# K worked in two halves, and weights by one masked multiply on VectorE, in a one-token attention kernel

## The chip, the cores and the metric

One core of one Trainium2 chip. The metric is device time of one execution in microseconds (us).

## The reference

```python
B, H, Sq, Skv, Dh = 8, 32, 1, 4096, 128          # q, k, v in bf16
scores = jnp.einsum('bhqd,bhkd->bhqk', q, k) * Dh ** -0.5
attn = softmax(scores, axis=-1)
return jnp.einsum('bhqk,bhkd->bhqd', attn, v)
```

One query row for each of 256 heads. K and V are read once each: 2 x 256 x 4096 x 128 x 2 bytes = 537 MB, against hardly any arithmetic per byte.

## The kernel before

A tile is 8 heads; 16 partitions hold one head, and each partition holds C = 256 of its rows. There are 32 tiles. One K or V tile is 8.4 MB, and three buffers of that size are shared by K and V in turn:

```python
kv_pool = ctx.enter_context(tc.tile_pool(name="kv_pool", bufs=SLOTS))     # SLOTS = 3
...
nc.sync.dma_start(buf[:, c0 : c0 + n, :], src[t, :, c0 : c0 + n, :])      # load(): all from one queue
```

V of a tile goes into the buffer that K of the same tile had, so its load is issued when TensorE has made the last sum over that K. K of tile t+1 goes into the buffer of V of tile t-2.

Scores: VectorE (DVE) multiplies K by q in place and folds the 128 products of a row once or twice; TensorE adds the rest up with an identity matrix, and VectorE reduces what is left.

```python
nc.vector.tensor_tensor(out=part, in0=part, in1=qb[:].to_broadcast([P, hi - lo, D]), op=ALU.mult)
nc.vector.tensor_tensor(out=part[:, :, 0 : D // 2], ..., op=ALU.add)           # 128 -> 64
if width_of(t, lo // UC) < D // 2:
    nc.vector.tensor_tensor(out=part[:, :, 0 : D // 4], ..., op=ALU.add)       # 64 -> 32
...
for s in range(n):                                      # sum_over_d(): a quarter of K at a time
    nc.tensor.matmul(ps[:], lhsT=ident[:],
        rhs=kt[:, u * UC : (u + 1) * UC, s * DS : (s + 1) * DS], ...)          # UC = 64, DS = 8
```

Weights: after the maximum, ScalarE (ACT) makes the exponentials, then eight copies, one per head, each scaled by a column that is 1 on the partitions of that head and 0 elsewhere.

```python
nc.scalar.activation(out=e[:], in_=sc[:], func=ACT.Exp, bias=nmax[:, 0:1], scale=scale, ...)
for g in range(G):
    nc.scalar.activation(out=w[:, :, g, :], in_=e_g, func=ACT.Copy, scale=mine[:, 0, g : g + 1])
```

Values: 64 matmuls of those weights with V. In tiles 1 to 29 they run in a loop for the tile before, behind the sums. The first and the last two tiles are handled apart, in quarters of K.

## Time and profile before

| | before |
|---|---|
| time, median of 3 | 1251.89 us (1251.55 to 1251.96) |
| load queue busy | 99.5% of 16 DMA engines' span |
| VectorE busy | 1021.9 us, 82% |
| TensorE busy, its weight loads not counted | 786.8 us, 63% |
| ScalarE busy | 166.1 us, 13% |
| VectorE's wait for K | 139.9 us in 28 waits |

### The profile page before, as it was taken

The page shows a single profiled execution, that of the slowest core. Times are in us where ns is not written, and L with a number is a line of the kernel's source. Part 1 is how long each engine was busy: PE and PEld are TensorE (multiplying, and loading weights), DVE is VectorE, ACT ScalarE, POOL GpSimd, SP SyncE. Part 2 cuts the span into 40 slices and gives each one's busy share as a digit, 9 for nine tenths or more (in the row PEclk, how much of TensorE's full clock was granted, in tenths as well). Part 3 has the DMA queues.
Part 4 walks back from the last instruction along what each step waited for, and adds up shares of the span by engine and source line. Part 5 has one row for each costly group of instructions (what it writes and reads, how often), then busy time and mean ns, then how long its engine had stood idle before and what let it go on. Part 6 is the DMA issues. An engine that isn't in the chain of part 4 may idle for free. (4 is left out here: it accounts for less than half of the span.)

```text
span 1250.2 us, 10842 instructions
## 1 busy us (share of the span) xinstructions
PE 786.8 (63%) x3116; PEld 299.6 (24%) x3116; DVE 1021.9 (82%) x495; ACT 166.1 (13%) x433; POOL 4.5 (0%) x24
## 2 busy tenths in 40 slices
PE   3366567666576655766558665577655776556755
PEld 1122123222232222322223222222222222212222
DVE  7887987878977789777798777987779877798783
ACT  0111011111011110111101111011110111101111
POOL 1000000000000000000000000000000000000000
PEclk9987788777888778877788777887778878779867
DMA  9999999999999999999999999999999999999997
GB/s 405 436 436 435 434 436 432 436 430 428 426 437 436 429 435 434 434 435 436 436 434 432 424 437 437 432 430 428 436 437 434 430 433 434 430 435 421 427 446 329
DMA packets 11432, 537.33 MB, mean 430 GB/s; under 512 B 1808, under 2 KB 2064, under 8 KB 2320
## 3 DMA queue, kind: packets, MB, share of 16 engines
q1 hardware_dynamic: 11072, 536.94, 99.5%
q8 instruction: 15, 0.25, 0.1%
q10 hardware_dynamic: 336, 0.07, 0.0%
q14 instruction: 9, 0.07, 0.0%
HBM read 536.94 MB, written 0.07 MB: 430 GB/s over the span
## 5 line engine op out<-in xcount | busy, mean ns | idle before, releaser
L191 DVE TENSOR_TENSOR kt<-kt,qb 128x8192 bf16<-128x8192 bf16 (+1 forms) x99 | 560.9, 5665 | 146.6 <-DMA kt<-in_k_dram 139.9
L211 PE MATMUL ps<-kt,ident 128*128 128x512 bf16 x800 | 278.4, 511 | 389.9 <-DVE kt L199 299.7
L294 PE MATMUL av<-vt,w 128*32 x1740 | 425.5, 397 | 4.6
L194 DVE TENSOR_TENSOR kt<-kt 128x4096 bf16<-128x4096 bf16 (+1 forms) x99 | 288.8, 2917 | 3.4
L294 PEld LDWEIGHTS av<-vt,w 128*32 x1740 | 173.4, 100 | 262.4 <-issue 119.5
L211 PEld LDWEIGHTS <-ident 128*128 128x128 bf16 x800 | 95.7, 120 | 565.4 <-issue 527.9
L223 DVE TENSOR_REDUCE sc<-ps 128x64 f32<-128x512 f32 x128 | 85.3, 685 | 54.0 <-PE ps L211 54.0
L248 ACT ACTIVATE e<-sc,nmax 128x256 bf16<-128x256 f32 x32 | 16.3, 508 | 706.7 <-DVE nmax L242 706.7
L255 ACT ACTIVATE w<-e,mine 128x256 bf16<-128x256 bf16 x256 | 105.6, 495 | 1.1
L199 DVE TENSOR_TENSOR kt<-kt 128x2048 bf16<-128x2048 bf16 x56 | 68.6, 1225 | 1.9
L351 ACT ACTIVATE comb<-av 32x512 bf16<-32x512 f32 (+1 forms) x32 | 18.8, 586 | 329.0 <-PEq L284 321.4
L280 PE MATMUL av<-vt,w 128*32 128x512 bf16 x116 | 47.2, 499 | 14.6 <-issue 13.1
L371 PE MATMUL op<-comb,pick 32*16 32x128 bf16 (+1 forms) x128 | 12.1, 213 | 20.7 <-ACT comb L351 20.7
L280 PEld LDWEIGHTS av<-vt,w 128*32 128x32 bf16 x116 | 6.9, 100 | 55.2 <-issue 55.2
L177 PE MATMUL qp<-qg,heads 8*128 8x128 bf16 x32 | 7.0, 217 | 16.7 <-ACT qg L175 16.7
L371 PEld LDWEIGHTS <-pick 32*16 32x16 bf16 (+1 forms) x128 | 8.7, 83 | 27.7 <-issue 27.3
L322 PE MATMUL av<-vt,w 128*32 128x512 bf16 x188 | 13.7, 418 | 2.3 <-DMA vt<-in_v_dram 2.3
L235 DVE TENSOR_REDUCE pmax<-sc 128x1 f32<-128x256 f32 x32 | 13.4, 420 | 1.1
L175 ACT ACTIVATE qg<-qh 8x128 bf16<-8x128 f32 x32 | 8.5, 266 | 33.5 <-PE qh L171 33.5
L171 PE MATMUL qh<-q_all,ident 128*8 128x128 bf16 x32 | 7.2, 225 | 8.7 <-DMA q_all<-in_q_dram 8.3
L179 ACT ACTIVATE qb<-qp 128x128 bf16<-128x128 f32 x32 | 8.9, 278 | 9.7 <-PE qp L177 9.7
L237 DVE TENSOR_SCALAR spread<-same,pmax 128x32 f32<-128x32 f32 x32 | 7.7, 242 | 1.1
(31 smaller groups left out, 47.7 us busy)
## 6 DMA issues: line engine op xcount, KB each, us to landing
kt<-in_k_dram SPq DMA_DIRECT2D x4, 4096.0 KB, 24.3
kt<-in_k_dram SPq DMA_DIRECT2D x4, 2048.0 KB, 13.0
vt<-in_v_dram SPq DMA_DIRECT2D x1, 4096.0 KB, 33.9
vt<-in_v_dram SPq DMA_DIRECT2D x1, 2048.0 KB, 38.5
vt<-in_v_dram SPq DMA_DIRECT2D x1, 1024.0 KB, 40.5
vt<-in_v_dram SPq DMA_DIRECT2D x1, 512.0 KB, 41.3
vt<-in_v_dram SPq DMA_DIRECT2D x31, 25.8
kt<-in_k_dram SPq DMA_DIRECT2D x29, 28.3
```

What stands on the lines that cost most here:

```text
L191: nc.vector.tensor_tensor(out=part, in0=part, in1=qb[:].to_broadcast([P, hi - lo, D]), op=ALU.mult)
L194: nc.vector.tensor_tensor(out=part[:, :, 0 : D // 2], in0=part[:, :, 0 : D // 2], in1=part[:, :, D // 2 : D], op=ALU.add,)
L199: nc.vector.tensor_tensor(out=part[:, :, 0 : D // 4], in0=part[:, :, 0 : D // 4], in1=part[:, :, D // 4 : D // 2], op=ALU.add,)
L211: nc.tensor.matmul(ps[:], lhsT=ident[:], rhs=kt[:, u * UC : (u + 1) * UC, s * DS : (s + 1) * DS], start=(s == 0), stop=(s == n - 1),)
L223: made = nc.vector.tensor_reduce(out=scs[t][:, u * UC : (u + 1) * UC], in_=sums.pop((t, u))[:], axis=AX.X, op=ALU.add)
L248: nc.scalar.activation(out=e[:], in_=sc[:], func=ACT.Exp, bias=nmax[:, 0:1], scale=scale, accum_out=esums[t // R][:, t % R : t % R + 1],)
L255: nc.scalar.activation(out=w[:, :, g, :], in_=e_g, func=ACT.Copy, scale=mine[:, 0, g : g + 1])
L280: pe.matmul(av, lhsT=wf[:, i * nw : (i + 1) * nw], rhs=vf[:, i * nv : (i + 1) * nv], **how)
L294: pe.matmul(av, lhsT=wf[:, bass.ds(ow + i * nw, nw)], rhs=vf[:, bass.ds(ov + i * nv, nv)], start=False, stop=False,)
L322: nc.tensor.matmul(avs[t][j * AG : (j + 1) * AG, :], lhsT=w[:, i, :, :], rhs=vt[:, c0 : c0 + CB, :], start=(i < TG), stop=(j not in group[ ...
L351: nc.scalar.activation(out=comb[0:n, :, :], in_=av[0:n, :, :], func=ACT.Copy)
L371: nc.tensor.matmul(ops[n][:], lhsT=pick[0:e, m, r, :], rhs=comb[0:e, m, :], start=(r == 0 and m == 0), stop=(r == R - 1 and m == CB - 1 an ...
```

## The change

Its intent is to give the looped tiles fewer and longer instructions: the second half of K becomes one multiply with one more fold, so that each half needs one tile of sums (`ps`, 128 x 512, written by TensorE) and one reduction; and the eight copies on ScalarE become one instruction on VectorE.

```diff
-        return D // 4 if u >= NU // 2 and 0 < t < NT - 3 else D // 2
+        return D // 8 if lo == C // 2 and 0 < t < NT - 3 else D // 2
...
+    mask = consts.tile([P, G], BF16, name="mask")
+    nc.gpsimd.tensor_copy(out=mask[:], in_=mine[:, 0, 0:G])
...
-        for g in range(G):
-            nc.scalar.activation(
-                out=w[:, :, g, :], in_=e_g, func=ACT.Copy, scale=mine[:, 0, g : g + 1]
-            )
+        e_g = e_g.rearrange("p i (o m) -> p i o m", o=1).to_broadcast([P, C // CB, G, CB])
+        own_g = mask[:].rearrange("p (o g q) -> p o g q", o=1, q=1)
+        nc.vector.tensor_tensor(
+            out=w[:], in0=e_g, in1=own_g.to_broadcast([P, C // CB, G, CB]), op=ALU.mult
+        )
...
             if loop:
-                sum_over_d(t, 0)
...
+                sum_over_d(t, 0, HALF)
+                product(t, HALF, C)
+                sum_over_d(t, HALF, C)
+                scores_of(t, 0, HALF)
...
                 values_loop(t - 1)
                 load("k", t + 1)
                 load("v", t)
+                scores_of(t, HALF, C)
```

More of the change, by code (lines that the diff above doesn't have):

```diff
@@ L43 @@
     scale = float(D) ** -0.5
-    UC = 64
-    DS = 512 // UC
-    NU = C // UC
+    BANK = 512
     CB = 4
@@ L180, in q_prep, with width_of @@
         qbs[t] = qb
-    def width_of(t, u):
-        return D // 4 if u >= NU // 2 and 0 < t < NT - 3 else D // 2
+    def width_of(t, lo):
+        return D // 8 if lo == C // 2 and 0 < t < NT - 3 else D // 2
     def product(t, lo, hi):
@@ L193, in product, with sum_over_d, scores_of @@
         )
-        nc.vector.tensor_tensor(
-            out=part[:, :, 0 : D // 2], in0=part[:, :, 0 : D // 2],
-            in1=part[:, :, D // 2 : D], op=ALU.add,
-        )
-        if width_of(t, lo // UC) < D // 2:
+        n = D
+        while n > width_of(t, lo):
+            n //= 2
             nc.vector.tensor_tensor(
-                out=part[:, :, 0 : D // 4], in0=part[:, :, 0 : D // 4],
-                in1=part[:, :, D // 4 : D // 2], op=ALU.add,
+                out=part[:, :, 0:n], in0=part[:, :, 0:n], in1=part[:, :, n : 2 * n], op=ALU.add
             )
     sums = {}
-    def sum_over_d(t, u):
+    def sum_over_d(t, lo, hi):
         kt = loads["k", t]
-        ps = ps_s.tile([P, UC, DS], F32, name="ps", tag="ps")
-        n = width_of(t, u) // DS
+        ps = ps_s.tile([P, BANK], F32, name="ps", tag="ps")
+        ds = BANK // (hi - lo)
+        n = width_of(t, lo) // ds
         for s in range(n):
             nc.tensor.matmul(
-                ps[:], lhsT=ident[:],
-                rhs=kt[:, u * UC : (u + 1) * UC, s * DS : (s + 1) * DS],
+                ps[:], lhsT=ident[:], rhs=kt[:, lo:hi, s * ds : (s + 1) * ds],
                 start=(s == 0), stop=(s == n - 1),
             )
-        sums[t, u] = ps
+        sums[t, lo] = ps
     scs = {}
-    def scores_of(t, u):
-        if u == 0:
+    def scores_of(t, lo, hi):
+        if lo == 0:
             scs[t] = sc_pool.tile([P, C], F32, name="sc", tag="sc")
+        ps = sums.pop((t, lo))[:].rearrange("p (c s) -> p c s", c=hi - lo)
         made = nc.vector.tensor_reduce(
-            out=scs[t][:, u * UC : (u + 1) * UC], in_=sums.pop((t, u))[:], axis=AX.X, op=ALU.add
+            out=scs[t][:, lo:hi], in_=ps, axis=AX.X, op=ALU.add
         )
-        if u == NU - 1:
+        if hi == C:
             behind_loop(made)
@@ L253, in weights_of @@
         e_g = e[:].rearrange("p (i m) -> p i m", m=CB)
-        for g in range(G):
-            nc.scalar.activation(
-                out=w[:, :, g, :], in_=e_g, func=ACT.Copy, scale=mine[:, 0, g : g + 1]
-            )
+        e_g = e_g.rearrange("p i (o m) -> p i o m", o=1).to_broadcast([P, C // CB, G, CB])
[3 more added lines that the diff above has]
+        )
         ws[t] = w
@@ L392, in store_of @@
             nc.scalar.dma_start(o_n[s, :, lo : u + 1, :], stages[s][:, lo : u + 1, :])
-    Q = C // 4
+    Q, HALF = C // 4, C // 2
     load("k", 0)
@@ L408 @@
                 load("v", t)
-            product(t, 0, 2 * Q if loop else Q)
+            first = HALF if loop else Q
+            product(t, 0, first)
             if not loop:
-                sum_over_d(t, 0)
+                sum_over_d(t, 0, first)
             if 0 < t - 1 <= LT:
@@ L419 @@
             if loop:
-                sum_over_d(t, 0)
-            else:
-                product(t, Q, 2 * Q)
-            sum_over_d(t, 1)
-            if not loop:
-                scores_of(t, 0)
-            product(t, 2 * Q, 3 * Q)
-            sum_over_d(t, 2)
-            if loop:
-                scores_of(t, 0)
-            scores_of(t, 1)
-            if t > 2 and t % R == 1:
-                recip_of(n)
-            product(t, 3 * Q, C)
-            sum_over_d(t, 3)
-            scores_of(t, 2)
-            if loop:
+                sum_over_d(t, 0, HALF)
+                product(t, HALF, C)
+                sum_over_d(t, HALF, C)
+                scores_of(t, 0, HALF)
+                if t > 2 and t % R == 1:
+                    recip_of(n)
                 values_loop(t - 1)
@@ L439 @@
                 load("v", t)
+                scores_of(t, HALF, C)
+            else:
+                product(t, Q, HALF)
+                sum_over_d(t, Q, HALF)
+                scores_of(t, 0, Q)
+                product(t, HALF, HALF + Q)
+                sum_over_d(t, HALF, HALF + Q)
+                scores_of(t, Q, HALF)
+                if t > 2 and t % R == 1:
+                    recip_of(n)
+                product(t, HALF + Q, C)
+                sum_over_d(t, HALF + Q, C)
+                scores_of(t, HALF, HALF + Q)
             if v_last:
                 values_of(t - 1, 0, C)
-            scores_of(t, 3)
+            if not loop:
+                scores_of(t, HALF + Q, C)
             weights_of(t)
```

## The prediction

> **What bounds the kernel now.** I read the page's busy shares first, then the slices and the DMA queues, then the waits, then one steady tile in the timeline. From the page:
>
> ```profile
> PE 786.8 (63%) x3116; PEld 299.6 (24%) x3116; DVE 1021.9 (82%) x495; ACT 166.1 (13%) x433; POOL 4.5 (0%) x24
> ...
> DMA  9999999999999999999999999999999999999997
> GB/s 405 436 436 435 434 436 432 436 430 428 426 437 436 429 435 434 434 435 436 436 434 432 424 437 437 432 430 428 436 437 434 430 433 434 430 435 421 427 446 329
> ...
> q1 hardware_dynamic: 11072, 536.94, 99.5%
> ```
>
> VectorE (DVE) is busiest of the compute engines, but the load queue fills 99.5% of the span of all 16 DMA engines, and never dips between the first slice and the last. K and V together are 537 MB; at the 434 GB/s of a steady slice one tile (8 heads, 16.8 MB of K and V) takes about 38.7 us, and 32 tiles take 1237 us of the 1250.2. The kernel is bound by its loads. A change in compute can cost time only if it makes a load be issued too late, and can save only in the few us outside the stream. VectorE's largest wait, of the waits view, agrees: it waits for K.
>
> ```profile
> DVE kt L191 <- DMA kt<-in_k_dram: 139.9, 28, 6.3
> ```
>
> How much room there is I read from one steady tile, in the timeline of VectorE and of SyncE's queue:
>
> ```profile
> 624.96 8.69 DVE L191 TENSOR_TENSOR kt<-kt,qb 128x16384 bf16<-128x16384 bf16 x1 [4.88 <-DMA kt<-in_k_dram]
> 633.69 4.42 DVE L194 TENSOR_TENSOR kt<-kt 128x8192 bf16<-128x8192 bf16 x1
> 638.03 4.42 DVE L191 TENSOR_TENSOR kt<-kt,qb 128x8192 bf16<-128x8192 bf16 x1
> 642.49 2.29 DVE L194 TENSOR_TENSOR kt<-kt 128x4096 bf16<-128x4096 bf16 x1
> 644.81 1.23 DVE L199 TENSOR_TENSOR kt<-kt 128x2048 bf16<-128x2048 bf16 x1
> ...
> 657.11 0.69 DVE L223 TENSOR_REDUCE sc<-ps 128x64 f32<-128x512 f32 x1 [1.35 <-PE ps L211]
> ...
> 663.67 8.69 DVE L191 TENSOR_TENSOR kt<-kt,qb 128x16384 bf16<-128x16384 bf16 x1 [4.89 <-DMA kt<-in_k_dram]
> ```
>
> ```profile
> 618.41 0.33 SPq L158 DMA_DIRECT2D vt<-in_v_dram  x1
> 635.26 0.33 SPq L158 DMA_DIRECT2D kt<-in_k_dram  x1
> 657.11 0.33 SPq L158 DMA_DIRECT2D vt<-in_v_dram  x1
> ```
>
> K lands at 624.96 and the next K at 663.67, 38.7 us on. The V load into this K's slot is issued at 657.11, 32.15 us after K landed, when TensorE's last sum over it is done. Loads are moved in order, each some 19.3 us, so that V's turn comes at 663.67: 6.6 us of slack. The K load is issued at 635.26 when the value loop ends, and its turn is 19.3 us after 624.96, at 644.3: 9 us of slack. VectorE is idle 4.9 us before each K, and 1.35 us before the last reduction.
>
> [...]8192 elements in 4.42 us, the 512-element reduction in 0.685 us. [...]The new sums read 4 bf16 (8 bytes) in a run where they read 8 before[...].
>
> **The change part by part, on VectorE's chain of one steady tile**, in us from K's landing. The first half is as before: 8.69 and 4.42, and the next product starts at 13.07.
>
> Second half, removed: twice (4.42 + 2.29 + 1.22) = 15.9. Added: one product of 16384 elements, 8.69; the fold to 64, 4.42; to 32 (128 rows by 32, 4096 elements as in the old quarter's fold), 2.29; to 16 (2048 elements), 1.22; together 16.6. So VectorE pays 0.7 for folding once more. But two reductions of 0.685 (1.28 as a pair) that stood between the products in before are gone from there: the last fold ends at 13.07 + 16.6 + small starts = 29.75, against 30.2 before (655.15 to 624.96).
>
> TensorE: the second half needs 16/4 = 4 matmuls of 512 columns in place of 2 x 4; of the first half 64/4 = 16 as before. The last group is again four[...], so the sums are done at 31.65 (32.15 before). V is therefore issued 0.5 us EARLIER, at a slack of 7. The value loop behind it and the K issue move by the same 0.5. Over the kernel 28 x 4 = 112 of the 800 matmuls go, about 57 us of busy time at 511 ns, all off the path.
>
> The end of the tile: the first half's reduction (0.69) runs while TensorE does the last sums. The second reduction starts at 31.67, and the maximum chain is unchanged: nmax starts 1.46 after it and takes 0.21, the exponential starts 1.77 after it, at 33.44, and its 0.51 and accumulator read 0.19 end at 34.05. Now VectorE, in order, must wait there for ScalarE: a new wait of about 0.8. Then the masked multiply[...]: (685 - 420) ns for 512 - 256 elements is 1.035 ns each, so 685 + 1536 x 1.035 = 2.27 us. [...]It ends at about 36.4. The next K comes at 38.7, so VectorE still has 2.3 us to spare. The weights are ready at 36.4, against 37.9 with eight copies of 0.41 start to start; nobody waits for them in the loop.
>
> Sum over the kernel for VectorE: 28 x 0.75 = +21; 58 reductions of 0.685 fewer, -40; 32 masks of 2.27, +73: busy from 1021.9 to about 1076 us (86%). ScalarE loses 105.6 us, 166 to about 61. None of it is on the path.
>
> **The two ends** are where a delay could show. Start: tile 1 is processed without waiting for K. Tile 0's mask multiply sits before its product, so this starts at 42.72 + 0.8 + 2.3 = 45.8, and V1 is issued at 77.5; its turn comes when K2 has landed, 80.95. Hidden, with 3.4 us left. The next product starts at about 82.2, 1.3 late, and the tile after that is on time again.
>
> End: K30 and K31 land in pieces and there VectorE does not wait for K. The mask of tile 29 delays tile 30 by 3.1, but tile 30 waited 3.88 us for TensorE's value loop at 1180.38, which swallows it. The mask of tile 30 delays tile 31 by 3.1: last sums at 1235.0 instead of 1231.87, weights at 1239.7 instead of 1237.56. TensorE's values of tile 30 and the copy and result behind them move equally, so values of tile 31 start near 1240.8 instead of 1238.56. The last V piece lands as before:
>
> ```profile
> 1238.56 1.89 PE L322 MATMUL av<-vt,w 128*32 128x512 bf16 x29
> ...
> 1241.62 1.89 PE L322 MATMUL av<-vt,w 128*32 128x512 bf16 x16 [1.09 <-DMA vt<-in_v_dram]
> 1244.14 0.61 PE L322 MATMUL av<-vt,w 128*32 128x512 bf16 x8 [0.63 <-DMA vt<-in_v_dram]
> 1245.37 0.40 PE L322 MATMUL av<-vt,w 128*32 128x512 bf16 x4 [0.62 <-DMA vt<-in_v_dram]
> ```
>
> The three waits for V here add up to 2.34 us, and the delay is 2.2 to 2.3: 1240.8 + 1.89 + 0.24 + 1.89 + 0.61 + 0.40 = 1245.8, where before ends at 1245.77. So the tail gains 0 to 0.5 us. Total: 1251.9 + 0 to 0.3; I say **1252.0**.
>
> **Rivals.** (a) VectorE becomes the bound: the mask multiply would have to take over 2.27 + 2.3 = 4.5 us, twice my estimate. At 5 us each steady tile would last 0.5 longer, 14 us in all less the 6.6 of slack: 1260. [...](b) The 8-byte runs slow the sums: [...]V's slack shrinks from 7 to 5, and VectorE's spare from 2.3 to 0.4. The time stays, but for some 2 us in the tail only if the quarters there were hit too; they keep 8-element runs. (c) Both at once[...]: perhaps 1256. (d) Faster: less work on VectorE, TensorE and ScalarE would only matter if one of them were the bound. [...]At most the tail, about 5 us after the last load, could shrink, and the change touches none of its steps. (e) The change takes nothing from HBM traffic, so the time of the stream may vary only as the rate does from run to run.
>
> **Range and chances.** The work gives 1251.9 to 1252.4[...]; (a) to (c) lengthen the upper side. 8 in 10: 1249.5 to 1255.0. A change of 2% is 25 us, more than any rival gives: faster 0.01, within 2% 0.97, slower 0.02.
>
> **What would show it.** The load queue again near 99.5%; the wait of VectorE for K down from 139.9 to about 65; a wait of VectorE for the exponential, 32 times, about 25 in sum; the mask group near 2.27 us each; V issued about 31.7 us after K lands, not 32.15; 688 sum matmuls at or below 511 ns; in the last 10 us no waits for V of any size. I am wrong if the queue shows gaps in the middle slices, if VectorE no longer waits for K, or if the mask takes over 4.5 us.

The forecast's sum came to 1251.9 + 0 to 0.3, said as 1252.0; terms on the way to it and to the range:

- The 2.5 us of spread in the range of 1249.5 to 1255.0, an assumption. The six executions of before in these rounds lie within 0.83 us (1251.43 to 1252.26).
- The length of the last four sums, 1.86 us as in before (1.87 at 655.21): 29.75 and this make the 31.65 that follows, with 0.04 of small starts. In rival (b) they take twice that.
- The masked multiply, which reads each value of the mask four times, at the pace of the reductions. 2.27 us is an estimate from their 685 ns for 512 elements and 420 for 256; the other candidate was the 1.225 us of before's fold of 2048. Which of them holds, before does not show.

Nor does before show what the 8-byte runs do to the sums, or that loads can go no faster than the 434 to 437 GB/s of 22 of its slices.

## The result, and the profile after

The changed kernel took 1251.71 us (median of 6, 1251.36 to 1252.17); before took 1251.72 in the same rounds (1251.43 to 1252.26). The ratio is 1.000, 95% interval 0.9987 to 1.0012. A ratio here is the mean time of one kernel's fast runs over that of the other's of the same rounds, so not quite the ratio of the medians.

The page of the changed kernel, its busy shares, slices and load queue (busy us and share of the span; tenths and GB/s in 40 slices; packets, MB, share):

```profile
PE 762.6 (61%) x3004; PEld 284.0 (23%) x3004; DVE 1083.8 (87%) x411; ACT 60.7 (5%) x177; POOL 4.7 (0%) x25
...
DMA  9999999999999999999999999999999999999997
...
q1 hardware_dynamic: 11072, 536.94, 99.5%
```

62 us more of VectorE, 105 us less of ScalarE, 24 less of TensorE, and the queue is as full as before. The waits of the changed kernel (engine and line that waited, for whom: us in all, times, longest) say what the added work displaced:

```profile
DVE kt L191 <- DMA kt<-in_k_dram: 63.4, 27, 3.3
DVE sc L221 <- PE ps L209: 53.6, 33, 5.7
DVE w L254 <- ACT e L246: 23.1, 32, 0.7
```

VectorE's wait for K, 139.9 before, has shrunk by 76.5, and a wait of 0.73 for the exponential, 32 times, is new. One steady tile of VectorE in the timeline (start, busy us; in brackets the idle time before, and what ended it), and the loads that SyncE's queue issued about it:

```profile
625.43 8.69 DVE L191 TENSOR_TENSOR kt<-kt,qb 128x16384 bf16<-128x16384 bf16 x1 [2.30 <-DMA kt<-in_k_dram]
634.15 4.42 DVE L197 TENSOR_TENSOR kt<-kt 128x8192 bf16<-128x8192 bf16 x1
638.50 8.68 DVE L191 TENSOR_TENSOR kt<-kt,qb 128x16384 bf16<-128x16384 bf16 x1
647.22 8.01 DVE L197 TENSOR_TENSOR kt<-kt 128x8192 bf16<-128x8192 bf16 x3
655.14 0.68 DVE L221 TENSOR_REDUCE sc<-ps 128x128 f32<-128x512 f32 x1
657.21 0.69 DVE L221 TENSOR_REDUCE sc<-ps 128x128 f32<-128x512 f32 x1 [1.38 <-PE ps L209]
...
659.61 2.29 DVE L254 TENSOR_TENSOR w<-e,mask 128x2048 bf16<-128x2048 bf16 x1 [0.73 <-ACT e L246]
664.15 8.69 DVE L191 TENSOR_TENSOR kt<-kt,qb 128x16384 bf16<-128x16384 bf16 x1 [2.25 <-DMA kt<-in_k_dram]
```

```profile
635.30 0.33 SPq L158 DMA_DIRECT2D kt<-in_k_dram  x1
657.20 0.33 SPq L158 DMA_DIRECT2D vt<-in_v_dram  x1
```

From K to K it is 38.7 us still. VectorE is idle 2.25 us before K, where it was 4.9. V is issued 657.20 - 625.43 = 31.77 us after K lands (32.15 before), a little earlier, and K at 9.9 us after it (10.3 before). The added work lies behind the point that releases V's load, where nothing waits for it.

The tail has lost its room. TensorE's last values in the timeline:

```profile
1241.05 1.89 PE L321 MATMUL av<-vt,w 128*32 128x512 bf16 x29
...
1242.88 2.32 PE L321 MATMUL av<-vt,w 128*32 128x512 bf16 x24
...
1245.48 0.40 PE L321 MATMUL av<-vt,w 128*32 128x512 bf16 x4 [0.28 <-DMA vt<-in_v_dram]
```

Before waited three times for V here, 2.34 us in all. 0.28 is left, and the last four matmuls start 0.11 us later than before did.

### The profile page after: what moved, and what is told of

It is laid out like the page before. It is cut to its first block, busy times and chain, and to the rows that moved or that the text cites. A ratio compares the mean times of both kernels' runs of the same rounds, so it can differ in the third digit from the quotient of the medians.

```text
span 1250.1 us, 10338 instructions
## 1 busy us (share of the span) xinstructions
PE 762.6 (61%) x3004; PEld 284.0 (23%) x3004; DVE 1083.8 (87%) x411; ACT 60.7 (5%) x177; POOL 4.7 (0%) x25
## 3 DMA queue, kind: packets, MB, share of 16 engines
q1 hardware_dynamic: 11072, 536.94, 99.5%
## 5 line engine op out<-in xcount | busy, mean ns | idle before, releaser
L191 DVE TENSOR_TENSOR kt<-kt,qb 128x16384 bf16<-128x16384 bf16 (+1 forms) x70 | 556.9, 7956 | 70.2 <-DMA kt<-in_k_dram 63.4
L209 PE MATMUL ps<-kt,ident 128*128 128x512 bf16 x688 | 256.5, 542 | 421.3 <-DVE kt L197 421.0
L197 DVE TENSOR_TENSOR kt<-kt 128x4096 bf16<-128x4096 bf16 (+1 forms) x126 | 382.6, 3037 | 4.3
L209 PEld LDWEIGHTS <-ident 128*128 128x128 bf16 x688 | 80.4, 125 | 587.5 <-DVE kt L197 445.7
L221 DVE TENSOR_REDUCE sc<-ps 128x128 f32<-128x512 f32 (+1 forms) x70 | 48.1, 687 | 53.6 <-PE ps L209 53.6
L254 DVE TENSOR_TENSOR w<-e,mask 128x2048 bf16<-128x2048 bf16 x32 | 73.4, 2293 | 23.1 <-ACT e L246 23.1
L240 DVE TRANSPOSE_TENSOR_REDUCE nmax<-spread 128x1 f32<-128x32 f32 x32 | 6.8, 212 | 1.1
```

Source lines behind the costliest of these rows:

```text
L197: nc.vector.tensor_tensor(out=part[:, :, 0:n], in0=part[:, :, 0:n], in1=part[:, :, n : 2 * n], op=ALU.add)
L209: nc.tensor.matmul(ps[:], lhsT=ident[:], rhs=kt[:, lo:hi, s * ds : (s + 1) * ds], start=(s == 0), stop=(s == n - 1),)
L221: made = nc.vector.tensor_reduce(out=scs[t][:, lo:hi], in_=ps, axis=AX.X, op=ALU.add)
L254: nc.vector.tensor_tensor(out=w[:], in0=e_g, in1=own_g.to_broadcast([P, C // CB, G, CB]), op=ALU.mult)
```

## The experiments

The theory: the stream of loads sets the time, and compute moves it only where it uses up the slack (VectorE's wait for K, V's early issue, the waits in the tail). One rival: the two parts of the change move the time in opposite ways and cancel. Another: whatever runs on VectorE is hidden. All kernels whose result is not said to be wrong were correct.

### One part alone

K in halves, with the eight copies on ScalarE kept:

```diff
-        e_g = e_g.rearrange(...).to_broadcast(...)
-        nc.vector.tensor_tensor(out=w[:], in0=e_g, in1=own_g..., op=ALU.mult)
+        for g in range(G):
+            nc.scalar.activation(out=w[:, :, g, :], in_=e_g, func=ACT.Copy, scale=mine[:, 0, g : g + 1])
```

> The half of the change on K alone, with the eight ScalarE copies kept. Theory (the load stream binds, compute only uses up slack): same time as both kernels, 1251.7 within 2 us, load queue at 99.5%; VectorE waits for K about 5 us a tile again (some 145 us in sum), V is issued 31.7 to 31.8 us after K lands. Rival (the two parts move the time in opposite ways and cancel): clearly faster than before, by more than 2 us.

Measured: 1250.92 us (1250.80 to 1251.08) against 1251.86 of before, ratio 0.9992, interval 0.9976 to 1.0009.

The masked multiply in the kernel before, K in quarters (the same edit the other way):

> The masked multiply alone, K still in quarters. Theory: same time, 1251.7 within 2 us; VectorE's wait for K falls to about 1.9 us a tile (4.9 less 0.73 of waiting for the exponential and 2.29 of multiply), some 55 us in sum; V issued 32.15 us after K lands, as before. Rival (the parts cancel): clearly slower than before, by more than 2 us.

Measured: 1252.58 us (1252.46 to 1252.75) against 1251.86, ratio 1.0005, interval 0.9989 to 1.0022. VectorE's wait for K, first of K in halves alone, then of the mask alone:

```profile
DVE kt L189 <- DMA kt<-in_k_dram: 149.6, 28, 6.5
```

```profile
DVE kt L193 <- DMA kt<-in_k_dram: 52.4, 27, 2.8
```

Both parts alone are within 0.1% of before, and the waits moved as expected: 139.9 to 149.6 with one, to 52.4 with the other. So no two large effects cancel. The medians do stand 0.9 below and 0.7 above before, in the direction of the rival, and none of the four runs of either overlaps with the seven of before; but both intervals hold 1, and neither difference is over the 2 us that would have meant it. Where it lies can be seen: the last V lands 0.9 us earlier in the profile of the first (the last four value matmuls start at 1244.46, in before at 1245.37), so it is in the stream itself. In the traces most tiles take 38.7 us and a few about 39.6. The packed traces show where. In the six profiles with a full queue (before, after, both parts alone, the fast mask and the doubled last tile below), between 105 and 1160 us, 318 times from one landing of a full K or V to the next were counted. In 224 of them no packet of the instruction queues (q8 and q14, which the page calls instruction; packets of 8 KB or more) began, and none took over 19.43 us. In the other 94 one did, and 27 of these took over 19.5 us, up to 20.4. So the long tiles are among those in which such a packet was moved. Over this stretch the loads of K in halves alone are together 1.0 us shorter than those of before, about the 0.9 looked for. That the packet lengthens the load is not tested, and why the other 67 were not longer stays open.

### More of the disputed work

The changed kernel with the masked multiply done twice, and three times, for every tile:

```diff
-        nc.vector.tensor_tensor(out=w[:], in0=e_g, in1=own_g..., op=ALU.mult)
+        for _ in range(2):      # 3 in the second
+            nc.vector.tensor_tensor(out=w[:], in0=e_g, in1=own_g..., op=ALU.mult)
```

> After with the masked multiply done twice, so 32 x 2.25 = 72 us more of VectorE. Theory: the changed kernel's VectorE waits 63.4 us for K in sum; that is used up and only what exceeds it shows, so +9 us: 1261, between 1257 and 1264; VectorE's wait for K near zero. Rival (VectorE's work is already on the path, each us counts): 1324. Rival (nothing on VectorE counts): 1251.7.

Measured: 1259.64 us (1259.13 to 1261.70), ratio to before 1.006 (1.0044 to 1.0077). VectorE's wait for K, and the start of TensorE's last values:

```profile
DVE kt L191 <- DMA kt<-in_k_dram: 1.3, 1, 1.3
```

```profile
1249.83 3.58 PE L322 MATMUL av<-vt,w 128*32 128x512 bf16 x32 [2.23 <-DVE w L255]
```

> After with the masked multiply done three times, 144 us more of VectorE. Theory: 144 less the 63.4 of waiting, +81: 1332, between 1326 and 1338; VectorE near 98% busy, no wait for K, the load queue falls to about 93% with gaps. So the first extra multiply costs 9 us and the second 72. Rival (each us counts from the start): 1396. Rival (nothing counts): 1251.7.

Measured: 1334.40 us (1334.28 to 1335.11), ratio 1.066 (1.0643 to 1.0678). The slices and the load queue of three times:

```profile
DVE  7899999999999999999999999999999999998985
...
GB/s 411 441 378 410 409 417 402 409 409 410 423 395 410 410 409 409 410 409 409 408 409 410 412 409 408 409 413 407 410 409 407 412 410 409 410 409 407 404 401 175
...
q1 hardware_dynamic: 11072, 536.94, 94.7%
```

The first 73 us of extra work on VectorE cost 8 us, the second 73 cost 75: it turns where the 63.4 us of waiting for K are used up. But the 63.4 us are not one store that any tile can draw on. In the profile of twice, VectorE starts on tile 29 only 3.1 us later than in the changed kernel (1133.22 against 1130.17); the end comes 9.9 us later (1260.0 against 1250.1), since tiles 29 to 31, which pay 2.3 us each, have no wait for K behind their multiply. Both rivals (each us counts; nothing counts) are out. One expectation missed: VectorE is 92% busy at three times, not 98%, for its waits for TensorE (52.5 us) and for the exponential (23.1) stay when the wait for K is gone. It is the bound at 92% busy.

### The tail

The multiply doubled in the last tile alone:

```diff
+        for _ in range(2 if t == NT - 1 else 1):
             nc.vector.tensor_tensor(out=w[:], in0=e_g, in1=own_g..., op=ALU.mult)
```

> After with the masked multiply doubled in the last tile alone, 2.25 us more at the one place where the changed kernel has almost no slack left (0.28 us of waits for V in the tail). Theory: the tail now starts its last values about 2 us later, and the end moves by 1.5 to 2.0 us: 1253.2 to 1253.7, and no wait of TensorE for V is left in the tail. Rival (the tail is set by the last V's landing whatever VectorE does): no change, within 0.3 us.

Measured: 1254.08 us (1252.79 to 1254.56) against 1251.84, ratio 1.0015 (1.0002 to 1.0029). The timeline of TensorE there:

```profile
1242.46 3.47 PE L322 MATMUL av<-vt,w 128*32 128x512 bf16 x32 [2.34 <-DVE w L255]
...
1245.87 2.54 PE L322 MATMUL av<-vt,w 128*32 128x512 bf16 x28
```

The end moved by 2.2 us (of the medians; 2.4 in the profiles) for 2.3 of work, so at this one place VectorE is on the path. It is somewhat over the range expected, though in this profile tile 31's sums were done 0.7 us earlier than in the changed kernel, so that its values began only 1.6 us later. The first line shows where the rest came from: TensorE stood idle 2.34 us for the weights, and the same 32 matmuls then took 3.47 us, where in the changed kernel they took 2.05 (1240.89 to 1242.94). Part of that was hidden, as no V had to be waited for afterwards.

### A faster form of the multiply

The mask stored four times over, so that no innermost step is zero:

```diff
-    mask = consts.tile([P, G], BF16, name="mask")
+    mask = consts.tile([P, G, CB], BF16, name="mask")
...
-        own_g = mask[:].rearrange("p (o g q) -> p o g q", o=1, q=1)
+        own_g = mask[:].rearrange("p (o g) m -> p o g m", o=1)
```

> After with the mask stored four times over, so that the multiply's second source has an innermost step of one and repeats a row of 32. [...]1.22 us each (as the fold of 2048 elements) in place of 2.293, 39 us of VectorE in all; if the broadcast in the middle of either source also costs, it stays at 2.29. Theory on the time: same, 1251.7 within 1 us, VectorE's wait for K up from 63 to about 97 us; the waits for V in the tail back to about 2 us. Rival (VectorE's path counts): up to 30 us faster.

Measured: 1251.41 us (1251.29 to 1251.90) against 1251.84, ratio 0.9998 (0.9985 to 1.0012). The group of the multiply (count; busy us, mean ns; idle before, releaser), of the changed kernel and of this one:

```profile
L254 DVE TENSOR_TENSOR w<-e,mask 128x2048 bf16<-128x2048 bf16 x32 | 73.4, 2293 | 23.1 <-ACT e L246 23.1
```

```profile
L257 DVE TENSOR_TENSOR w<-e,mask 128x2048 bf16<-128x2048 bf16 x32 | 39.2, 1225 | 23.1 <-ACT e L249 23.1
```

1225 ns against 2293: the mask's innermost step of zero alone nearly doubled the multiply's time. Without it, the multiply takes as long as a fold of 2048 elements (1225 ns in the changed kernel, L197). The e operand, repeated in rows of four in both forms, does not keep it from that. This run shows the effect of the step for this one shape. The time stays; VectorE waits 93.1 us for K. That is 29.7 more, where the multiplies take 34.2 less; the last three tiles, 3.2 of it, have no such wait that could grow. The tail waits for V come to 2.2 us again.

### With the loads off the path

To see what the change is worth as compute, half of each looped V is neither loaded nor used. The results are wrong. All work on K, scores and weights is as it was; TensorE's value matmuls in the loop are halved too. Four kernels got this edit: before, after, K in halves alone, and the mask alone; a fifth is after with the fast mask.

```diff
-LOOP = 6
+LOOP = 7
-    NV = C // CB
+    NV = C // CB // 2
-        for n in cuts.get((kind, t), [C]):
+        for n in cuts.get((kind, t), [C // 2] if kind == "v" and t < NT - 3 else [C]):
```

> Before, with only half of each V loaded and used in the looped tiles (wrong result on purpose), to take the load stream off the path: 12.6 MB a tile is 29.0 us at 434 GB/s, below the compute chain. Theory: now VectorE's chain binds, 33.8 us a tile (38.7 less 4.9 idle): about 1110 us, with no wait for K in the steady tiles. Rival (some other thing than loads sets 38.7 us a tile): above 1200.

> The changed kernel with the same half V (wrong result on purpose). Theory: VectorE's chain is 36.4 us a tile (38.7 less 2.25), so about 1184 us, 6 to 7% slower than before with half V: the change as compute is a loss that the loads hide. Rival (the change costs nothing on VectorE's chain, or gains): equal to or faster than before with half V.

> Half V (wrong result on purpose) with K in halves and the eight ScalarE copies kept. Theory: the chain is 33.35 us a tile (38.7 less the 5.35 of idle before K with K in halves alone) against 33.8, so some 12 us less than before with half V (1105.6): 1092 to 1096. This part is a gain where VectorE binds. Rival (folding once more costs 0.7 us of VectorE a tile and is a loss): 1115 or more.

> Half V (wrong result on purpose) with the masked multiply alone, K in quarters. Theory: 2.29 of multiply and 0.73 of waiting for the exponential on each of 32 tiles, 95 us more than before with half V: 1195 to 1201, and the two parts add up to the change (1184.1). Rival (only the multiply counts, the wait would be there anyway): 1178.

> Half V (wrong result on purpose) with the changed kernel and the mask stored four times over, at 1.225 us a multiply. Theory: 32 x 1.07 = 34 us less than the changed kernel with half V: 1148 to 1152, still some 4% slower than before with half V, for VectorE still waits and multiplies where ScalarE copied beside it. Rival (the fast multiply makes the change pay): under 1105.

| half V, loads off the path | time, us | against before with half V | a steady tile, mean of 23 |
|---|---|---|---|
| before | 1105.57 (1105.27 to 1105.61) | | 33.74 us |
| after | 1184.13 (1183.22 to 1184.51) | +78.6 | 36.37 |
| K in halves alone | 1095.16 (1094.93 to 1095.84) | -10.4 | 33.35 |
| mask alone | 1194.17 (1193.99 to 1194.67) | +88.6 | 36.76 |
| after, fast mask | 1151.84 (1151.78 to 1152.48) | +46.3 | 35.30 |

The two ends of a steady tile, that is VectorE's product on one K and on the next, in before and after with half V:

```profile
514.91 8.67 DVE L190 TENSOR_TENSOR kt<-kt,qb 128x16384 bf16<-128x16384 bf16 x1
548.68 8.67 DVE L190 TENSOR_TENSOR kt<-kt,qb 128x16384 bf16<-128x16384 bf16 x1
```

```profile
518.63 8.69 DVE L190 TENSOR_TENSOR kt<-kt,qb 128x16384 bf16<-128x16384 bf16 x1
...
555.01 8.68 DVE L190 TENSOR_TENSOR kt<-kt,qb 128x16384 bf16<-128x16384 bf16 x1
```

No wait is noted before these products: VectorE now binds, 33.7 us a tile in before and 36.4 after, and the load queue is no longer full (89.5% and 83.5%). The change is a loss of 7.1% there (1184.13 over 1105.57, of the medians), and in the real kernel the loads hide it. Its parts have opposite signs and add up: -10.4 + 88.6 = 78.2. K in halves gains 0.39 us a tile; its one more fold costs 0.76 (21.2 us more in the products and folds of 28 tiles, 939.5 in after's page against 918.3 in before's), but the reductions are half as many and no longer stand between the products. The mask costs 3.02 us a tile, 2.29 of work and 0.73 of waiting; over 31 tiles that would be 94, and 5 come back at the end, where TensorE's last values ran quicker in that run (1.89 and 2.53 us for 29 and 28 of them, against 2.88 and 4.37, with 0.88 of waiting for V between them). The three estimates of after, K in halves and the fast mask held (the last at the edge of its range); of the other two, before came out 4 us below its "about 1110", and the mask just below its range of 1195 to 1201, well above its rival's 1178.

No version beats both kernels by more than the noise. K in halves alone has the lowest median of all, 0.9 us below before, and its interval holds 1.

## Why the prediction was right

- **The bound.** Confirmed: the queue stays at 99.5%, 38.7 us a tile, and with half of each V a tile falls to 33.7 us. That edit takes away loads and value matmuls at once. But the value loop of the steady tile ended, and issued K, 9 us before K's turn, and the queue was full; so it was the loads that set the 38.7.
- **VectorE's chain.** V's issue was put at 31.65 us after K, it was 31.77; the mask at 2.27, it took 2.293 (that it would not take the fold's 1.225 was the assumption until the run with the fast mask); the idle time before K at 2.3, it was 2.25; the wait for K at about 65, it was 63.4; the one for the exponential at about 25, it was 23.1.
- **VectorE's busy sum** was put at 1076 and was 1083.8. The step that was too small is "58 reductions of 0.685 fewer, -40": the group fell only from 85.3 to 48.1, 37.2, as before's pairs overlapped (1.28 for two). Some 4.5 more is overlap between groups, which the page counts once: the DVE groups of before add up to 1034.1 for 1021.9 busy, those of after to 1091.5 for 1083.8. It lay off the path.
- **TensorE.** 688 sum matmuls, as said, but 542 ns each, not "at or below 511". The 57 us of busy time that were to go are a misreading: 511 ns is the mean length of matmuls that overlap, and the 800 of before are busy for 278.4 us, 348 each. The group fell by 21.9 us, to 256.5. In the steady tiles none of it is on the path. Sixteen sums with 16-byte runs in before, two times, and sixteen with 8-byte runs in after:

```profile
212.00 5.30 PE L211 MATMUL ps<-kt,ident 128*128 128x512 bf16 x16 [1.17 <-DVE kt L194]
638.17 3.61 PE L211 MATMUL ps<-kt,ident 128*128 128x512 bf16 x16 [1.17 <-DVE kt L194]
```

```profile
211.67 5.32 PE L209 MATMUL ps<-kt,ident 128*128 128x512 bf16 x16 [1.50 <-DVE kt L197]
1143.38 3.64 PE L209 MATMUL ps<-kt,ident 128*128 128x512 bf16 x16 [1.40 <-DVE kt L197]
```

  Both kernels have quick ones and slow ones (up to 6.5 us), and these pairs agree within 0.03 us. So rival (b), 8-byte runs at twice the time, is out. Over the whole kernel sixteen took 5.0 us in before and 5.5 in after; what part the 8 bytes have in that is not shown. What makes one slow is open: in before the same pause of 1.17 us stands in front of both. A long pause does go with slow sums in tile 29's second sixteen: 9.42 us idle and 6.28 for the sums in after, 7.80 and 5.55 with the fast mask, 6.59 and 5.09 with K in halves alone. The granted clock (the share of full speed that TensorE was let run at) was 0.777 to 0.805 in the executions of after, 0.795 to 0.813 in those of before. Rivals (c) and (d) had it fall or rise, with reasons that no run shows.
- **The two ends.** Start: product 1 at 45.8, it was 45.87; V1 at 77.5, it was 77.64. End: tile 30 was to be 3.1 us late and swallowed in TensorE's wait; it was 4.25 late at 1167.36, and 1.4 late after the wait. The prediction had counted the mask alone, but tile 29 folds only once: its second half is now summed by those slow sixteen in one go (6.28 us), where in before eight (3.57) were left. So tile 31 started 4.2 late instead of 3.1, and its weights came at 1240.77 instead of 1239.7. The values still began about when predicted (the 29 at 1241.05, 2.5 later than in before; 1240.8 had been said), since the values of tile 30 went a little quicker (4.08 us against 4.61) and ScalarE, free of copies, copied their result 0.12 us after they ended (1240.18 after 1240.06), where in before it came to that 1.35 us after (1237.72 after 1236.37). Here the prediction was right by two errors that met.
- **Rival (a)**, over 4.5 us for the mask, is what three times the mask made true: 6.95 us, 1334.4. Its sum, 0.5 us a tile "less the 6.6 of slack", was too small: for 6.95 us it gives about 1313. The slack of the loads did not come off: tile 29 starts 69 us later than in the changed kernel, where 28 times the 2.4 us above the room of 4.57 make 67. And tiles 29 to 31 pay in full.

## What to carry to other kernels

Where a load queue is full, as here at 99.5%, find the instruction that releases the next load and count the us from there to the queue's turn. Work put behind that point was free here until the engine's wait for data was used up (73 us more cost 8), and then cost in full (the next 73 cost 75). Where that wait is missing, as in the last tiles here, work costs nearly in full from the start (2.2 us for 2.3). Take away some of the loads to learn what a change is worth as compute: here it was a loss of 78.6 us that the loads hid, and it came out when half of each V was left out. Eight small copies on an idle engine can be cheaper than one instruction on the busy one (with half V the mask alone cost 88.6 us), above all if that must also wait for the idle one's result in the middle of its order (0.73 us of the 3.02 a tile).
